# A decode step's last weight load cut into lines, and x added earlier on TensorE

## The chip, the cores and the metric

The kernel runs on one core of one Trainium2 chip, as one program. The metric is the device time of one execution in microseconds (us); the time of a kernel is the median of several executions. A separate, profiled execution gives the trace: which instruction ran when on which engine, when transfers were issued and when they landed, and the clock that TensorE was granted. TensorE does the matmuls, VectorE, ScalarE and GpSimd the elementwise work, and SyncE issues the transfers. Sixteen DMA engines carry them; a transfer is cut into packets, and each engine that takes part writes a closing packet of 4 bytes that counts up the transfer's semaphore.

## The reference

One decode step of two attention layers and two gated layers for a batch of 4 rows x of 512 numbers, all in bf16. Cut to what matters:

```python
def A(x, k_cache, v_cache, wq, wo):        # 32 query heads, 8 key heads, the last 2048 keys
    q = (x @ wq) split into heads
    p = softmax(q @ k.T * Dh ** -0.5)
    return (p @ v) joined @ wo

def B(x, w_gate, w_up, w_down):            # D = 512, F = 1792
    h = sigmoid(x @ w_gate) * (x @ w_up)
    return h @ w_down

x = x + A(layernorm(x)); x = x + B(layernorm(x))
x = x + A(layernorm(x)); x = x + B(layernorm(x))
```

Both rounds use the same caches and weights. The change lies in the last line's B: in the load of w_down, and in the place where x is added to h @ w_down.

## The kernel before, in words

The kernel writes down its work as a list of operations (`P.op`, line 52), each with its engine, an assumed duration, and the tiles that it reads and writes. `_schedule` (line 92) then gives each engine its order, by assumed times; in the second half of the program TensorE's operations keep the order in which they were written (`P.chain`, line 1622), and SyncE's transfers always do. `_assign_sync` (line 180) puts in the semaphore waits; the transfers go round 24 semaphores.

Nearly all transfers go from HBM into a large SBUF area, `arena`, cut into slots of 4 KB a partition. `load` and its kin append to a list of loads; `fill` issues from that list as soon as slots come free (`done`, line 469), and `need` (line 464) makes sure that a load has been issued before its user. The loads therefore run far ahead of the work, in one fixed order on one queue. The last ones are the gated layer's: two loads each of w_gate and w_up, and then w_down.

w_down has 1792 rows, laid out as 14 "lines" for each of 128 partitions (`wd_d`, line 319): partition p holds rows 14p to 14p + 13, and a block (a, b) of lines a to b - 1 is one transfer with one run of (b - a) KB for each partition. `bounds_of` (line 520) gives the blocks: in the last layer (0, 8), (8, 12) and (12, 14), in this order.

The last layer is `glu` with `last=True` (line 1445). Its steps, with their names:

- `glwg1_c` and `glwu1_c` (line 1484): for each quarter c of D, four matmuls of xn's 4 rows against 448 columns; quarters 0 and 1 come from the first load of the matrix, 2 and 3 from the second. The profile counts each of these pairs as 8 matmuls.
- gate and up are turned on VectorE (line 1496) and become hT, the transposed h (line 1518), by way of an exponential on ScalarE.
- `x_rows` (line 1457): GpSimd writes an identity into `prow` (line 1461), and four f32 matmuls (`xrow`, line 1468) write x's rows into the PSUM bank that will gather the result, with `start=True`. x is thus added by the accumulation.
- `kwI` (line 1522): two products of 448 columns into a bank that nobody reads. Such `keep_op`s (line 792) only keep TensorE busy.
- `gd1_a` (line 1533): for each line of a block four matmuls, one for each 128 columns, that add into that bank. Block (0, 8) has 32 of them, (8, 12) 16 and (12, 14) 8.
- four casts (line 1544), two on ScalarE and two on VectorE, and the transfer of the 4 result rows to HBM.

Of the kernel before, what the change touches and what calls it, by code (L numbers as in the profile page):

```python
# [254 lines left out]
class _SlotPool:  # L255
# [16 lines left out]
    bw_8k=421.0, bw_4k=409.0, bw_3k=405.0, bw_1k=347.0,  # L272
# [6 lines left out]
def build(nc, A_x, A_k, A_v, A_wq, A_wo, B_wg, B_wu, B_wd, out, cfg=None):  # L279
# [6 lines left out]
    NG = len(GROUPS)  # L286
# [38 lines left out]
    with es:  # L325
# [51 lines left out]
        def slot_ap(s):  # L377
            if s == SIDE:
                return side[:, 0:SLOT]
            return arena[:, s * SLOT:(s + 1) * SLOT]  # L380
# [7 lines left out]
        def tok(s):  # L388
            return [("slot", s), ("slot", s + 1)]
# [79 lines left out]
        def done(name):  # L469
            left[name] -= 1  # L470
            if left[name] == 0:
                s = where.pop(name)
                if name in on_free:
                    on_free[name](s)
                else:
                    pool.release(s)
                fill()
# [24 lines left out]
        def load(name, n_use, rate, part):  # L502
            left[name] = n_use

            def emit(s):
                src = part[1]
                dst = tile_ap(s)[:, 0:part[0]]
                if len(src.shape) == 3 and not part[2]:
                    dst = dst.rearrange("p (f n) -> p f n", f=src.shape[1])
                dma(str(name), dst, src, w=tok(s), rate=rate)  # L510
            loads.append((name, emit))
# [7 lines left out]

        def bounds_of(k):  # L520

            return [(0, 3), (3, 7), (7, 11), (11, NFC)] if k < NG else bounds[:-1] + [(bounds[-1][0], NFC - 2), (NFC - 2, NFC)]

        LAYERS = NG + 1

# [30 lines left out]
        def load_glu(k):  # L556
            for nm, src, two in (("wg", wg_d, wg_p), ("wu", wu_d, wu_p)):
                if k == 0:
                    for c in range(NC):
                        load_half((nm, c, k), src[:, c, :], "bw_3k", F,  # L560
                                  (((WR, 0), (Y, 0), (SP, 0), (Y, 1)), ((WQ, 0), (Z, 0), (WR, 0), (Y, 0)))[nm == "wu"][c])
                    continue
                for cc in range(NC // 2):
                    load((nm, cc, k), 2, "bw_8k", (2 * F, two[:, cc, :], False))
            for n, (a, b) in enumerate(bounds_of(k)):
                if k == 0:
                    load_half(("wd", a, k), wd_d[:, a:b, :].rearrange("p k n -> p (k n)"), "bw_4k", (b - a) * D,
                              ((SP, 0), (Y, 1), (WQ, 0), (Z, 0))[n])
                else:
                    load(("wd", a, k), 1, "bw_8k", ((b - a) * D, wd_d[:, a:b, :], False))  # L570


        STASH = SB + PBS
# [871 lines left out]
        def glu(k, b0, b1, add=None, last=False):  # L1445
# [11 lines left out]
            def x_rows():  # L1457
                xts = [("xT", b) for b in range(NB)]
                idf = prow[:, 256:512].bitcast(F32)
                P.op("gpsimd", "idf", 500.0,  # L1460
                     lambda g: g.affine_select(idf, one[:, 0:1].broadcast_to([128, 128]), [[1, 128]], ALU.is_equal, 0.0,
                                               base=0, channel_multiplier=-1),
                     r=[("one",)], w=[("prow",)])

                def e_x(pe):
                    last_ = None
                    for g in range(NC):
                        last_ = pe.matmul(ps[32 * g:32 * g + NB, PBS[0], 0:128], xT[:, g * NB:(g + 1) * NB], idf,
                                          start=True, stop=False, skip_group_check=True)
                    return last_  # L1470
                P.op("tensor", "xrow", 1200.0, e_x, r=xts + [("prow",)], w=[("orow",)], banks=(PBS[0],))
# [3 lines left out]
            for n, nm in enumerate(("wg", "wu")):  # L1475
                for c in range(NC):
                    name = (nm, c if k == 0 else c // 2, k)
                    s = need(name)

                    def e_g(pe, c=c, s=s, n=n):  # L1480
                        last = None
                        src = slot_ap(s) if k == 0 else tile_ap(s)[:, c % 2 * F:(c % 2 + 1) * F]
                        for g in range(4):
                            last = pe.matmul(ps[32 * g:32 * g + NB, gub[n], 0:NF], xn[:, c * NB:(c + 1) * NB],  # L1484
                                             src[:, g * NF:(g + 1) * NF], start=(c == 0), stop=(c == NC - 1),
                                             skip_group_check=True)
                        if k == 0 and c < NC - 1:
                            add_zeros(pe, 3 if c == 2 - 2 * n else 2, WB, NF)
                        return last
                    P.op("tensor", "gl%s%d_%d" % (nm, k, c), 4 * tm["pe_row"], e_g,  # L1490
                         r=(stok(s) if k == 0 else tok(s)) + [("xn",)], w=[("gu", n)], banks=(gub[n],))
                    done(name)
                if n == 0:
                    variance()
                P.op("vector", "gt%s%d" % (nm, k), c_dve(NF),
                     lambda v, n=n: v.transpose(ebuf[:, 0:NF],  # L1496
                                                ps[:, gub[n], 0:NF].rearrange("p (x k) -> p k x", k=NFC)),
                     r=[("gu", n)], w=[("e", 0), ("e", 1)], banks=(gub[n],))

                if n == 0:  # L1500
                    P.op("vector", "gs%d" % k, c_dve(NH),
                         lambda v: v.tensor_tensor(egv, tv, lnr[:, 0:nb].unsqueeze(1).broadcast_to([128, NFC, nb]), ALU.mult),
                         r=[("e", 0), ("e", 1), ("lnr", 0)], w=[("eg",), ("op", 0), ("op", 1)])
                    P.op("scalar", "gex%d" % k, c_act(NH),
                         lambda a: a.activation(eg[:, 0:NH], eg[:, 0:NH], ACTF.Exp, scale=-1.0),
                         r=[("eg",)], w=[("eg",)])
                    P.op("vector", "ga%d" % k, c_dve(NH),
                         lambda v: v.scalar_tensor_tensor(egv, egv, 1.0, lnd[:, 0:nb].unsqueeze(1).broadcast_to([128, NFC, nb]),
                                                          ALU.add, ALU.mult),
                         r=[("eg",), ("lnd",)], w=[("eg",)])  # L1510
                    P.op("vector", "gr%d" % k, c_dve(NH) + 60.0,
                         lambda v: v.reciprocal(eg[:, 0:NH], eg[:, 0:NH]), r=[("eg",)], w=[("eg",)])
# [5 lines left out]
                 lambda v: v.tensor_tensor(hT[:, 0:NH].rearrange("p (k b) -> p k b", b=NB), tv, egv, ALU.mult),  # L1518
                 r=[("e", 0), ("e", 1), ("eg",), ("op", 0), ("op", 1)], w=[("hT",)] + hts)
            if last:  # L1520
                x_rows()
                keep_op("kwI", 2, SB[0], 0, 448)
                for (a, b) in bounds_of(k):
                    name = ("wd", a, k)
                    s = need(name)

                    def e_d(pe, a=a, b=b, s=s):
                        last_ = None
                        src = tile_ap(s)
                        for fc in range(a, b):  # L1530
                            for g in range(NC):
                                o = (fc - a) * D + g * 128
                                last_ = pe.matmul(ps[32 * g:32 * g + NB, PBS[0], 0:128], hT[:, fc * NB:(fc + 1) * NB],
                                                  src[:, o:o + 128], start=False, stop=(fc == NFC - 1),
                                                  skip_group_check=True)
                        return last_
                    P.op("tensor", "gd%d_%d" % (k, a), (b - a) * 200.0, e_d,
                         r=tok(s) + [("hT",)] + hts, w=[("orow",)], banks=(PBS[0],))
                    done(name)
                orow = ebuf[0:NB, 0:half].bitcast(BF16)  # L1540
                for g in range(NC):
                    eng, f = ("scalar", "copy") if g % 2 == 0 else ("vector", "tensor_copy")
                    P.op(eng, "oc%d" % g, c_dve(128),
                         lambda e, g=g, f=f: getattr(e, f)(orow[:, g * 128:(g + 1) * 128], ps[32 * g:32 * g + NB, PBS[0], 0:128]),
                         r=[("orow",)], w=[("oc", g)], banks=() if g else (PBS[0],))
                dma("out", out_d, orow, w=[("out_dram",)], r=[("oc", g) for g in range(NC)], rate="bw_1k", nbytes=NB * D * 2,
                    sem=("out",))
                return
# [148 lines left out]
```

## Time and profile before

| what | value |
|---|---|
| median of 3 runs | 176.15 us (176.08 to 176.18) |
| profiled execution, its own time | 176.3 us |
| its span, first to last instruction | 174.6 us |
| TensorE (PE) busy | 114.9 us, 66% |
| VectorE (DVE) busy | 105.9 us, 61% |
| ScalarE (ACT), GpSimd (POOL) busy | 34.0 us, 23.1 us |
| read from HBM | 69.37 MB, 397 GB/s over the span |
| SyncE's transfer queue (q1) | 12344 packets, 97.0% of the 16 engines' span |
| mean granted TensorE clock | 0.98 |

How to read it: the profile's page cuts the span into 40 slices of 4.4 us and prints for each the busy share in tenths; the DMA row is the mean share of the 16 DMA engines, so that 0.32 means that about five of them work. The chain that ended last is followed back from the last instruction: each piece was released by the one in front of it. In a timeline row stand start, duration, engine, line, operation, the tiles written and read, and, in brackets, how long the engine idled before and what ended that. A matmul's duration contains its way through the array, so that matmuls in a row overlap.

### The profile page before, as it was taken

Reading aid. Unit: us, or ns where it says so; the run is one execution under the profiler, and the core shown is the slowest. Engines: PE = TensorE matmul, PEld = TensorE weight load, DVE = VectorE, ACT = ScalarE, POOL = GpSimd, SP = SyncE. Lnnn points to the kernel's source line nnn. Section 1 sums busy time; section 2 is a strip of 40 time slices with the busy share of each in tenths; the row PEclk is TensorE's granted clock in tenths of the full one; section 3 lists DMA queues with packets and bytes.
Section 4 is the critical chain, followed back from the end, with each engine's and each line's share of the span. In section 5 each row is a group of like instructions: output and inputs, shape, how many; then the busy total and the mean of one; then the engine's idle time right before and its main releaser. Section 6 shows DMA issues by size and latency. Waiting matters only on the chain.

```text
span 174.6 us, 3997 instructions
## 1 busy us (share of the span) xinstructions
PE 114.9 (66%) x1686; PEld 58.6 (34%) x1698; DVE 105.9 (61%) x262; ACT 34.0 (19%) x89; POOL 23.1 (13%) x92
## 2 busy tenths in 40 slices
PE   0536237167557092569788788767958999879853
PEld 0203012013434051243467552243323434446311
DVE  6407997994866938469323732316598999751531
ACT  2002022312212103011021010102233545430101
POOL 6100010101100101001010000002011543442000
PEclk9999999999999999999999999999999999999975
DMA  5999999999999999999999999999999999999970
GB/s 189 420 428 430 422 420 420 408 423 420 420 419 409 424 420 420 420 412 421 420 408 425 412 395 407 407 409 405 407 413 417 422 417 420 417 424 420 415 319 26
DMA packets 12370, 69.64 MB, mean 399 GB/s; under 512 B 1336, under 2 KB 1472, under 8 KB 6336
## 3 DMA queue, kind: packets, MB, share of 16 engines
q1 hardware_dynamic: 12344, 69.38, 97.0%
q8 instruction: 13, 0.21, 0.5%
q14 instruction: 5, 0.04, 0.1%
q10 hardware_dynamic: 8, 0.00, 0.0%
HBM read 69.37 MB, written 0.00 MB: 397 GB/s over the span
## 4 chain that ended last, share of the span: by engine, by line
DMA 71%; PE 11%; DVE 7%; SPq 6%; issue 1%; ACT 1%; POOL 0%; DVEq 0%
DMA arena<-in_A_v_cache_dram 49%; DMA arena<-in_B_w_down_dram 15%; SPq L400 6%; DMA side<-in_A_wq_dram 4%; DMA arena<-in_B_w_up_dram 4%; PE ps L783 2%; PE ps L1088 2%; DVE arena L595 1%; PE ps L986 1%; PE ps L1091 1%; PE ps L1181 1%; DVE small L1001 1%; ACT side L1016 1%; PE ps L1289 1%; DVE arena L1191 1%
## 5 line engine op out<-in xcount | busy, mean ns | idle before, releaser
L956 DVE STREAM_TRANSPOSE arena<-arena 128x1024 f32<-128x1024 f32 x32 | 37.0, 1205 | 0.1
L986 PE MATMUL ps<-arena,side 128*32 128x512 bf16 x256 | 23.3, 494 | 0.3
L1001 DVE TENSOR_REDUCE small<-ps 128x1 f32<-128x512 f32 x16 | 10.9, 679 | 15.8 <-PE ps L986 15.8
L783 PE MATMUL ps<-perm 128*128 128x448 bf16 (+1 forms) x65 | 18.5, 397 | 1.0 <-DVE side L1496 0.8
L1016 ACT ACTIVATE side<-ps,small 128x512 bf16<-128x512 f32 x16 | 11.0, 687 | 35.7 <-PE ps L1115 18.5
L973 PE MATMUL ps<-small,perm 128*128 128x512 bf16 x16 | 7.7, 482 | 12.0 <-DVE arena L956 11.3
L1088 PE MATMUL ps<-side,arena 128*128 128x64 bf16 x320 | 11.3, 192 | 4.0 <-DMA arena<-in_A_v_cache_dram 4.0
L1091 PE MATMUL ps<-side,arena 128*128 128x8 bf16 x256 | 8.1, 168 | 8.8 <-DMA arena<-in_A_v_cache_dram 8.7
L949 ACT CAST side<-ps 128x256 bf16<-128x256 f32 x16 | 5.9, 371 | 33.6 <-PE ps L986 26.6
L1088 PEld LDWEIGHTS ps<-side,arena 128*128 128x128 bf16 x320 | 10.2, 97 | 6.3 <-DMA arena<-in_A_v_cache_dram 6.3
L1031 ACT CAST side<-ps 128x512 bf16<-128x512 f32 x16 | 9.4, 587 | 12.6 <-PE ps L1289 2.9
L1045 POOL CAST small<-small 128x1 bf16<-128x1 f32 x9 | 1.7, 188 | 76.0 <-ACT side L1016 76.0
L1091 PEld LDWEIGHTS ps<-side,arena 128*128 128x128 bf16 x256 | 7.4, 104 | 11.6 <-DMA arena<-in_A_v_cache_dram 9.0
L986 PEld LDWEIGHTS ps<-arena,side 128*32 128x32 bf16 x256 | 6.3, 108 | 11.7 <-issue 8.7
L897 PE MATMUL ps<-arena,xn 128*4 128x512 bf16 x60 | 6.5, 498 | 4.2 <-DMA arena<-in_A_wq_dram 4.2
L1105 DVE TENSOR_TENSOR onb<-ps,rinv 128x16 bf16<-128x16 f32 x9 | 1.7, 185 | 11.4 <-PE ps L1088 10.8
L944 PE MATMUL ps<-side,eyew 32*128 32x64 bf16 x64 | 5.4, 212 | 4.3 <-ACT side L949 2.4
L1036 DVE STREAM_TRANSPOSE side<-side 128x256 f32<-128x256 f32 x16 | 6.9, 433 | 2.0 <-ACT side L1031 1.8
L1181 PE MATMUL ps<-arena,side 128*32 128x512 bf16 x112 | 7.3, 380 | 0.8 <-ACT side L1016 0.4
L783 PEld LDWEIGHTS ps<-perm 128*128 128x128 bf16 x65 | 5.9, 110 | 5.3 <-issue 2.9
L1496 DVE STREAM_TRANSPOSE side<-ps 128x448 f32<-128x448 f32 x4 | 2.6, 651 | 7.9 <-PE ps L1484 7.9
L1484 PE MATMUL ps<-arena,xn 128*4 128x448 bf16 x60 | 4.7, 360 | 3.1 <-DMA arena<-in_B_w_up_dram 2.7
(138 smaller groups left out, 151.1 us busy)
## 6 DMA issues: line engine op xcount, KB each, us to landing
arena<-in_A_v_cache_dram SPq DMA_DIRECT2D x26, 1024.0 KB, 16.6
arena<-in_A_k_cache_dram SPq DMA_DIRECT2D x16, 1024.0 KB, 24.9
arena<-in_A_wq_dram SPq DMA_DIRECT2D x4, 1024.0 KB, 7.8
arena<-in_A_wo_dram SPq DMA_DIRECT2D x3, 1024.0 KB, 26.6
arena<-in_A_v_cache_dram SPq DMA_DIRECT2D x5, 512.0 KB, 8.6
arena<-in_A_wq_dram SPq DMA_DIRECT2D x5, 512.0 KB, 6.7
arena<-in_B_w_up_dram SPq DMA_DIRECT2D x4, 448.0 KB, 6.1
arena<-in_B_w_gate_dram SPq DMA_DIRECT2D x2, 896.0 KB, 20.7
```

Source lines behind the costliest of these rows:

```text
L400: o = P.op("sync", name, 0.0, lambda e, dst=dst, src=src: e.dma_start(dst, src), r=r, w=w, dma_bytes=nbytes, dma_rate=tm[rate])
L783: last = pe.matmul(dst, weights, src, start=False, stop=False, skip_group_check=True)
L956: P.op("vector", "T%d_%d" % (h, t), c_dve(1024), lambda v, v32=v32: v.transpose(v32, v32), r=[("slot", 4 * h + t)], w=[("slot", 4 * h + t)])
L973: last = pe.matmul(ps[:, bank, :], perm[:, :], msk_m[:, :].unsqueeze(1).broadcast_to([128, 256, 2]), start=True, stop=False)
L986: last = pe.matmul(ps[32 * gi:32 * gi + 32, bank, :], qbd[:, q0:q0 + 32], kt[:, cp // 2, cp % 2, jh * NJ:(jh + 1) * NJ, :], start=False, s ...
L1001: lambda v: v.tensor_reduce(nmax[:, k2:k2 + 1], ps[:, bank, :], AXX, ALU.max),
L1016: lambda a: a.activation(prow[:, :].rearrange("p (m x t) -> p m x t", x=32, t=2), ps[:, bank, :].rearrange("p (m t x) -> p m x t", x=32, t ...
L1031: P.op("scalar", "pc" + tag, c_act(512), lambda a: a.copy(prow[:, :], ps[:, pb, :]), r=[("ppb", pb)], w=[("prow",)], banks=(pb,))
L1036: P.op("vector", "pt" + tag, c_dve(256), lambda v: v.transpose(et, prow[:, :].bitcast(F32)), r=[("prow",)], w=[("e", k2)])
L1088: last = pe.matmul(ps[:, ob, o:o + 64], v, ef[:, j % 2, at - at % 64:at - at % 64 + 64], start=(j == 0), stop=(j == 2 * NJ - 1), skip_grou ...
L1091: last = pe.matmul(ps[:, ob, bp * 8:bp * 8 + 8], v, ev[:, j % 2, j % 16 // 2, x0:x0 + 8], start=(j == 0), stop=(j == 2 * NJ - 1))
L1181: last = pe.matmul(ps[32 * g:32 * g + 32, ob, :], ew[:, g, mq, t], src.rearrange("p (m t d) -> p t m d", t=2, d=128)[:, t], start=(n == 0) ...
```

## The change

- The last layer's block (12, 14) becomes two blocks, (12, 13) and (13, 14), loaded in this order behind (8, 12).
- Block (13, 14) is loaded as two transfers: partitions 0 to 123 and partitions 124 to 127. The second has a token of its own, `wdb`, and takes over the first one's dependences, so that it waits for nothing else.
- TensorE works the blocks in the order (0, 8), (8, 12), (13, 14), (12, 13); the matmuls of line 13 wait for both of its parts.
- `x_rows` moves from behind hT to the place between the first and the second load of w_up, and four warm-keeping products (`kwJ`) go behind it.
- `kwI` has three products instead of two.

```diff
-            return [(0, 3), (3, 7), (7, 11), (11, NFC)] if k < NG else bounds[:-1] + [(bounds[-1][0], NFC - 2), (NFC - 2, NFC)]
+            return [(0, 3), (3, 7), (7, 11), (11, NFC)] if k < NG else bounds[:-1] + [(bounds[-1][0], NFC - 2), (NFC - 2, NFC - 1), (NFC - 1, NFC)]
...
+                elif b < NFC:
+                    load(("wd", a, k), 1, "bw_8k", ((b - a) * D, wd_d[:, a:b, :], False))
                 else:
-                    load(("wd", a, k), 1, "bw_8k", ((b - a) * D, wd_d[:, a:b, :], False))
+                    left["wd", a, k] = 1
+
+                    def emit(s):
+                        first = dma("wd%da" % a, slot_ap(s)[0:124, 0:D], wd_d[0:124, a, :], w=tok(s), rate="bw_1k")
+                        rest_ = dma("wd%db" % a, slot_ap(s)[124:128, 0:D], wd_d[124:128, a, :], w=[("wdb",)], rate="bw_1k")
+                        rest_.deps.update(first.deps)
+                    loads.append((("wd", a, k), emit))
...
                     done(name)
+                    if last and n and c == 1:
+                        x_rows()
+                        keep_op("kwJ", 4, SB[0], 0, 448)
...
             if last:
-                x_rows()
-                keep_op("kwI", 2, SB[0], 0, 448)
-                for (a, b) in bounds_of(k):
+                keep_op("kwI", 3, SB[0], 0, 448)
+                for (a, b) in bounds_of(k)[:-2] + bounds_of(k)[:-3:-1]:
...
-                                                  src[:, o:o + 128], start=False, stop=(fc == NFC - 1),
+                                                  src[:, o:o + 128], start=False, stop=(fc == NFC - 2),
...
-                         r=tok(s) + [("hT",)] + hts, w=[("orow",)], banks=(PBS[0],))
+                         r=tok(s) + [("wdb",)][:b == NFC] + [("hT",)] + hts, w=[("orow",)], banks=(PBS[0],))
```

## The prediction

> **What bounds the kernel now.** I read the head of the page first, then the chain that ended last from 140 us on, then the stretches around the end with their DMA share, then the timeline of the last ten microseconds.
>
> The page says that transfers fill the span, and that the queue which fetches instructions runs beside the loads:
>
> ```profile
> DMA  5999999999999999999999999999999999999970
> ...
> q1 hardware_dynamic: 12344, 69.38, 97.0%
> q8 instruction: 13, 0.21, 0.5%
> ...
> q10 hardware_dynamic: 8, 0.00, 0.0%
> ```
>
> The chain from 140 us on hangs on the w_down loads and then on the last 24 matmuls of line 1533:
>
> ```profile
> 144.13 26.99 DMA arena<-in_B_w_down_dram
> 171.12 0.04 issue
> 171.16 0.60 PE ps L1533 x16
> 171.76 0.04 issue
> 171.80 0.41 PE ps L1533 x8
> 172.21 0.02 issue
> 172.23 0.28 DVE side L1544
> ```
>
> The stretches (after the times come PE, PEld, DVE, ACT and POOL busy, granted clock, DMA share, GB/s) show how the transfers run out:
>
> ```profile
> 164.33:167.74 3.41, 1.65 (x30) 0.65 (x26) 1.59 (x4) 0.72 (x4) 0.00 (x0) 1.00 1.02 419
> ...
> 166.00:167.60 1.60, 0.14 (x4) 0.10 (x8) 0.72 (x2) 0.14 (x1) 0.00 (x0) 1.00 1.02 413
> 167.60:168.80 1.20, 1.20 (x17) 0.38 (x10) 0.61 (x1) 0.00 (x0) 0.00 (x0) 0.56 0.84 329
> 168.80:169.60 0.80, 0.64 (x2) 0.00 (x0) 0.26 (x2) 0.00 (x0) 0.00 (x0) 0.50 0.54 218
> 169.60:171.20 1.60, 1.06 (x36) 0.78 (x40) 0.00 (x0) 0.00 (x0) 0.00 (x0) 0.50 0.32 125
> ```
>
> From 169.6 to 171.2 the share is 0.32: about 5 of the 16 DMA engines still work while 11 are done. The trace records every completion. The 16 of load (8, 12) come at 167.98, 167.99, 168.11, 168.15, 168.44, 168.70, 169.22, 169.49, 169.51, 169.56, 169.71 and, for the late five, 170.93 to 171.12. Those of load (12, 14) end at 170.34 for eleven and 171.55 to 171.75 for the same five. The five are late because each carried two of the 13 instruction packets (16 KB, 1.02 to 1.11 us each, which move an engine's completions by about 1.5 us). So the last load is waited for on five engines, and the other eleven have 1.2 to 3.1 us to spare.
>
> The granted clock fell to half at 167.74, after a TensorE gap:
>
> ```profile
> 165.27 0.55 PE L1484 MATMUL ps<-arena,xn 128*4 128x448 bf16 x8
> ...
> 167.46 0.69 PE L1484 MATMUL ps<-arena,xn 128*4 128x448 bf16 x8 [1.64 <-DMA arena<-in_B_w_up_dram]
> ...
> 167.92 0.65 PE L1468 MATMUL ps<-side,xT 128*4 128x128 f32 x8
> ...
> 168.51 0.93 PE L783 MATMUL ps<-perm 128*128 128x448 bf16 x2
> ...
> 171.16 1.02 PE L1533 MATMUL ps<-arena,rinv 128*4 128x128 bf16 x24 [0.21 <-DMA arena<-in_B_w_down_dram]
> ...
> 172.91 0.34 SPq L400 DMA_DIRECT2D out_dram<-side  x1
> ```
>
> **The change, part by part.** The profiled execution took 176.3 us (span 174.6 and 1.7 around it); the three runs shown have a median of 176.15. I work in the span and take the saving off the median.
>
> *x and the warm-keeping matmuls.* The eight x passes took 0.65 us at half clock; four products of 448 columns took 0.93 us at full clock (the group at 152.93). Together at most 1.58 us; the gap from 165.82 to 167.46 holds 1.64. Should they run over by a tenth, the last up matmuls, the transpose (0.65) and hT (0.22) move by that tenth: hT stood ready at 169.10 and TensorE waited for load (0, 8) until 169.92, so 0.8 us of cover hides it. Taking x off its old place and making kwI three (at half clock 0.93 for two, so about 1.3) ends TensorE's work near 169.45, before 169.92. Cost zero, gain zero on the path; the identity that x needs was written by GpSimd at 155.97. What can come of it is the clock. The 3.41 us up to the fall had TensorE busy for 1.65; all such stretches before, back to 82.4 us, had 2.18 or more and kept full clock. With about 1.2 us more in it, this stretch has some 2.8, so the fall should not come at 167.74. But the next stretch, at full clock, has up matmuls 0.5, kwI 0.7 and the first w_down matmuls 0.6 and waits otherwise, again some 1.8 of 3.4: a fall before the last matmuls is as likely as not.
>
> In the Trainium skill, "TensorE: Matmul & The Clock Gate", section "What's actually happening", the gate watches a free-running window of 3413 ns. By it the fall lies elsewhere in each execution; the 3.41 us above agree, and the sum below holds for either clock.
>
> *The last load in parts.* A load of 128 lines gives each engine an equal share: the last one 8 packets of 2 KB, 80 ns from start to start. Line 12 alone is 8 packets of 1 KB; packets of 1 KB are seen only in the load of x, where the closing packet starts 40 ns after the data packet did. So the five late engines end 8 x 0.040 = 0.32 us earlier: 171.12 + 0.63 (now) becomes 171.12 + 0.32 = 171.44, if nothing of line 13 falls to them.
>
> How many engines take the 124 lines, no row of this trace shows. x's four lines made 8 packets on q10 (the row above), four of data and four closing ones: four engines, one line each. Bounds: spread over all 16, the late five carry 8 more packets (171.44 + 0.33 = 171.77, nothing gained); on four engines, each carries 31, 1.24 us. I take four, nearest to x's row.
>
> Which four decides. The first weight load starts on eight engines at 1.81 to 1.90 us, right behind x's packets, and on eight others at 2.60 or later. Of the first eight, four finish their first packet in 0.36 to 0.80 us and four in 1.11 to 1.23. I take the quick four to be those that had just carried x: two of them begin 11 ns after two of x's four closing packets end. Followed load by load through the completions, they stand at 168.44, 169.22, 169.49 and 169.71 at load (8, 12), none among the late five. The slowest then ends line 12 at 170.04, its 31 packets at 171.29, and its one packet of the 4-line part at 171.34: hidden behind 171.44, by only 0.1 us. Two further issues on SyncE (0.33 each) lie far ahead: its last load issue ended at 152.14, and only the output is queued behind them.
>
> The Trainium skill, "DMA: Bandwidth & Descriptors", section "Why a DMA increments its semaphore by 16 and not by 1", gives the largest divisor up to 16, on the lowest-numbered engines: four for 124 lines and the same four for 4. By its rule the sum is the one taken here; by an even spread it would be 176.2.
>
> *The end on TensorE.* The 16 matmuls of (8, 12) still start at 171.16. Behind them stand four of line 13 (they wait for both parts), then four of line 12. At half clock the rows give rounds of four at 107 ns and 0.31 for the last (8 took 0.41, 16 took 0.60, 32 took 1.02): six rounds make 5 x 0.107 + 0.31 = 0.85, ending at 172.01 instead of 172.21. At full clock a pair of weight load and matmul starts every 25 ns (16 in 0.55 at 157.20) and the last takes about 0.22: 23 x 0.025 + 0.22 = 0.80, ending at 171.96. So 0.20 to 0.25 us of the 0.31 that the loads give; the rest is lost because TensorE is now behind. The lower end is a gain of 0; the upper is 0.45, should the last matmuls start at 14 ns (the eight at the end of before) and wait for 171.49 alone. Casts, output and its landing follow unchanged.
>
> Sum: x and kwI 0; issues 0; loads -0.31; TensorE's backlog +0.08: -0.23. **176.15 - 0.23 = 175.92 us.**
>
> **The rivals.**
>
> *Both ends freed.* TensorE keeps full clock and its pairs go closer than 25 ns, so that the loads alone end it: 171.49 + 0.27 instead of 172.21, about 175.7. For it: the filled gap. Against it: the row of 25 ns, and the thin stretch from 168.7 on.
>
> *The split does nothing.* 124 lines go over all engines, or line 13's four engines end just after the late five and TensorE, which asks for line 13 first, holds line 12 behind it: 176.1 to 176.25. For it: my margin of 0.1 us, and TensorE's order. Against it: x's eight packets.
>
> *Slower: one of the four is a late one.* My identification rests on first-packet times and on following engines through crossings. If one of the late five carries line 13, its parts land at 171.12 + 0.32 + 1.25 + 0.06 = 172.75, the eight matmuls end at 172.79 + 0.41 = 173.20 instead of 172.21, and the time is 177.15. It begins to cost when one of the four completes load (8, 12) after 169.81, and costs over 0.2% from 170.48 on. A transfer on fewer engines does the same: on two, 62 packets take 2.5 us from 169.8 and end near 172.3, giving 176.6. For it: 31 packets on one engine are 1.24 us where eight took 0.64, five of sixteen engines are late, and no record here names an engine. Against it: the two starts right behind x's closing packets.
>
> **How the numbers follow.** The forecast has 0.50 (own range 175.78 to 176.1), both ends freed 0.15, nothing done 0.11, slower 0.24. 0.2% is 0.35 us, about what a measurement of this kernel can tell from no change. Faster than 175.80: 0.15 and 0.07 of the forecast's. Within: 0.43 and 0.11. Slower than 176.50: 0.24. The first three cases hold 0.76, so the range must reach into the slow case: 175.6 to 177.2.
>
> **What would show it.** Right: the late five completions of line 12 near 171.45, both parts of line 13 complete before that, on engines that were not late; in the stretch from 169.6 to 171.2 a DMA share of 0.4 to 0.55 rather than 0.32; x's matmuls at 165.9 and full clock past 167.74; the last matmul's end near 171.95. Wrong: a part of line 13 landing after 171.6 with TensorE's four matmuls waiting for it; sixteen completions spread for the 124 lines; or last matmuls that start with the landing at 171.49 and gain more than 0.35 us.

## The result, and the profile after

The changed kernel takes 176.55 us (median of 22 runs, 176.32 to 176.82), the kernel before, run beside it, 176.25 us (22 runs, 176.08 to 176.43). The ratio is 1.0016, with a 95% interval of 1.001 to 1.0023: slower by 0.30 us, where 0.23 us faster had been forecast. The time lies in the forecast's range of 175.6 to 177.2, but it moved the other way.

The profiled execution took 176.82 us (span 175.1, mean granted clock 0.986; before 176.3, 174.6 and 0.98). Its page, the rows of the clock, of the DMA share and of the queues:

```profile
PEclk9999999999999999999999999999999999999995
DMA  4999999999999999999999999999999999999970
...
q1 hardware_dynamic: 12480, 69.38, 96.6%
q8 instruction: 13, 0.21, 0.5%
```

The packet count says how many closing packets line 13 has. Block (12, 14) was 128 packets and 16 closing ones, 144. Line 12 alone is again 144. Line 13 is 128 packets of data and one closing packet for each engine of each part: with four engines for each part 4 + 4, so 136 more than before. 12344 + 136 = 12480, the number in the q1 row; the 124 lines spread over all sixteen would have made 12492. That the eight closing packets are four and four, the completions further down show.

The chain of the changed kernel that ended last, its end:

```profile
152.23 1.14 SPq L400
153.38 0.05 issue
153.42 18.75 DMA arena<-in_B_w_down_dram
172.17 0.14 issue
172.31 0.41 PE ps L1543 x8
172.74 0.28 DVE side L1554
173.02 0.33 DVEq L1666
```

It no longer runs through load (8, 12) and 16 matmuls: it hangs on one w_down transfer that lands at 172.17, and only eight matmuls follow. They start at 172.31, where the last eight of before started at 171.80; everything behind them is as long as it was. So the half microsecond between the two profiled executions lies in what lands last.

The stretches (after the times: PE, PEld, DVE, ACT and POOL busy, granted clock, DMA share, GB/s):

```profile
164.33:167.74 3.41, 2.77 (x46) 1.10 (x34) 1.58 (x4) 0.72 (x4) 0.00 (x0) 1.00 1.01 415
...
167.60:168.80 1.20, 1.16 (x11) 0.24 (x11) 0.65 (x1) 0.00 (x0) 0.00 (x0) 1.00 0.87 331
168.80:169.60 0.80, 0.00 (x0) 0.00 (x0) 0.22 (x1) 0.00 (x0) 0.00 (x0) 1.00 0.68 227
169.60:171.20 1.60, 1.02 (x32) 0.73 (x32) 0.00 (x0) 0.00 (x0) 0.00 (x0) 0.64 0.37 135
171.20:171.60 0.40, 0.06 (x5) 0.06 (x8) 0.00 (x0) 0.00 (x0) 0.00 (x0) 0.50 0.06 21
```

The clock is full to 168.80 and beyond, where it was 0.56 in the third of these stretches before. The DMA share is higher where three of line 13's engines work (0.68 against 0.54), and then hardly more than before: 0.37 against 0.32 from 169.60 on. From 171.20 to 171.60 it is 0.06: one engine of sixteen.

The timeline of the last ten microseconds:

```profile
165.72 0.39 PE L1476 MATMUL ps<-side,xT 128*4 128x128 f32 x8
...
166.04 0.93 PE L791 MATMUL ps<-perm 128*128 128x448 bf16 x4
...
167.53 0.55 PE L1492 MATMUL ps<-arena,xn 128*4 128x448 bf16 x8 [0.56 <-DMA arena<-in_B_w_up_dram]
...
168.02 0.74 PE L791 MATMUL ps<-perm 128*128 128x448 bf16 x3
...
170.17 1.02 PE L1543 MATMUL ps<-arena,rinv 128*4 128x128 bf16 x32 [1.41 <-DMA arena<-in_B_w_down_dram]
...
171.54 0.60 PE L1543 MATMUL ps<-arena,rinv 128*4 128x128 bf16 x16 [0.35 <-DMA arena<-in_B_w_down_dram]
...
172.31 0.38 PE L1543 MATMUL ps<-arena,rinv 128*4 128x128 bf16 x8 [0.17 <-DMA arena<-in_B_w_down_dram]
...
173.42 0.27 SPq L400 DMA_DIRECT2D out_dram<-side  x1
```

x's matmuls and the four products fill the gap in front of the last up piece, as the forecast had it. At the end TensorE is not behind: after the 16 matmuls of (8, 12) it waits again, and then works line 13 and line 12 together.

The completions, one for each engine that takes part, in order of time (us, from the trace); the bar stands in front of the late engines, of which one falls behind only between the first two rows:

```
load (0, 8)     166.85 166.86 166.99 167.05 167.34 167.35 167.38 168.01 168.19 168.24 168.32 168.90 | 169.84 169.87 170.11 170.12
load (8, 12)    168.14 168.15 168.27 168.34 168.62 168.63 168.67 169.29 169.54 169.60 170.43 | 171.00 171.05 171.22 171.32 171.49
line 12         168.49 168.50 168.59 168.66 168.99 169.04 169.09 169.71 169.94 170.00 170.73 | 171.29 171.51 171.52 171.76 171.77
line 13, 0-123  169.95 170.44 170.60 171.99
line 13, 124-   170.13 170.61 170.78 172.17
```

Four completions for each part. Three of the four engines are done long before the late five. The fourth is the eleventh in the row of load (8, 12), at 170.43 and not among the late five: its 31 packets start 42.5 ns apart, and 31 of these (1.32 us) before its completion at 171.99 lies 170.67, near the eleventh of line 12 at 170.73 and far from the tenth and the twelfth. Its one packet of the small part is counted at 172.17, 0.40 us behind the last of line 12.

### The profile page after: what moved, and what is told of

Same layout as the page of the kernel before. It is cut to its first block, busy times and chain, and to the rows that moved or that the text cites. A ratio compares the mean times of both kernels' runs of the same rounds, so it can differ in the third digit from the quotient of the medians.

```text
span 175.1 us, 4010 instructions
## 1 busy us (share of the span) xinstructions
PE 115.0 (66%) x1691; PEld 58.9 (34%) x1703; DVE 105.9 (60%) x262; ACT 33.9 (19%) x89; POOL 22.9 (13%) x92
## 3 DMA queue, kind: packets, MB, share of 16 engines
q1 hardware_dynamic: 12480, 69.38, 96.6%
## 4 chain that ended last, share of the span: by engine, by line
DMA 43%; DVE 31%; PE 20%; issue 2%; SPq 1%; ACT 1%; DVEq 0%
DMA arena<-in_A_v_cache_dram 19%; DVE arena L964 12%; DMA arena<-in_B_w_down_dram 11%; PE ps L994 7%; DMA arena<-in_A_wq_dram 6%; DVE small L1009 4%; DMA arena<-in_B_w_up_dram 4%; DMA side<-in_A_wq_dram 4%; PE ps L981 2%; DVE small L1013 2%; PE ps L791 2%; PE ps L1096 2%; DVE arena L1199 2%; DVE side L1044 2%; DVE side L1017 2%
## 5 line engine op out<-in xcount | busy, mean ns | idle before, releaser
L981 PEld LDWEIGHTS ps<-small,perm 128*128 128x128 bf16 x16 | 1.6, 100 | 13.9 <-DVE arena L964 12.6
```

The source lines that it names most:

```text
L981: last = pe.matmul(ps[:, bank, :], perm[:, :], msk_m[:, :].unsqueeze(1).broadcast_to([128, 256, 2]), start=True, stop=False)
```

## The experiments

The theory is that the loss is this fourth engine. Its rivals: the moved x and the extra products cost something; one more transfer with its wait costs by itself; the order on TensorE, line 13 ahead of line 12, holds finished work back. The later kernels vary how many engines share line 13. The table has the median, that of the kernel before measured beside it, the ratio with its interval, and from the profiled execution the last landings (us) of load (8, 12), of line 12 and of line 13.

| kernel | us | before | ratio (95%) | (8, 12) | line 12 | line 13 |
|---|---|---|---|---|---|---|
| changed kernel | 176.55 | 176.25 | 1.0016 (1.001 to 1.0023) | 171.49 | 171.77 | 172.17 |
| x_only | 176.33 | 176.29 | 1.0001 (0.9992 to 1.001) | 170.92 | 171.55, one block | 171.55, one block |
| split_only | 176.64 | 176.29 | 1.0018 (1.001 to 1.0027) | 171.30 | 171.70 | 172.05 |
| whole_lines | 176.24 | 176.29 | 0.9999 (0.999 to 1.0008) | 171.15 | 171.52 | 171.81 |
| line12_first | 176.46 | 176.29 | 1.0012 (1.0003 to 1.002) | 171.44 | 171.80 | 171.90 |
| four_early | 176.38 | 176.33 | 1.0004 (0.9994 to 1.0013) | 171.53 | 171.81 | 171.80 |
| cut_123 | 176.30 | 176.33 | 0.9999 (0.999 to 1.0008) | 171.40 | 171.68 | 171.41 |
| cut_123_12_first | 176.38 | 176.33 | 1.0003 (0.9993 to 1.0012) | 171.40 | 171.70 | 171.41 |
| cut_121 | 176.68 | 176.33 | 1.0022 (1.0013 to 1.0031) | 171.41 | 171.71 | 172.11 |
| cut_119 | 177.05 | 176.31 | 1.0035 (1.0023 to 1.0048) | 171.46 | 171.76 | 172.49 |

### x moved, w_down as before (x_only)

Against the kernel before, only the second half of the diff is kept:

```diff
+                    if last and n and c == 1:
+                        x_rows()
+                        keep_op("kwJ", 4, SB[0], 0, 448)
...
-                x_rows()
-                keep_op("kwI", 2, SB[0], 0, 448)
+                keep_op("kwI", 3, SB[0], 0, 448)
```

> Only x and the warm-keeping products are moved; w_down comes in its old three blocks. Theory L (the end is set by the slowest of the four engines that carry line 13): nothing is left of the loss, 176.2 to 176.3 beside a before of 176.25. Theory X (the earlier x passes and the seven products get in the way of the up matmuls): the loss of 0.3 us stays, 176.5 to 176.6.

176.33 against 176.29, neither a loss nor a gain that can be measured: the moved x is not the cause. The clock stayed full until 172.51 in the profiled execution, and the last eight matmuls start 0.05 behind the landing at 171.55, as before. The timeline of x_only:

```profile
167.75 0.74 PE L783 MATMUL ps<-perm 128*128 128x448 bf16 x3
...
169.80 0.62 PE L1535 MATMUL ps<-arena,rinv 128*4 128x128 bf16 x32 [1.31 <-DMA arena<-in_B_w_down_dram]
...
170.96 0.40 PE L1535 MATMUL ps<-arena,rinv 128*4 128x128 bf16 x16 [0.55 <-DMA arena<-in_B_w_down_dram]
...
171.60 0.28 PE L1535 MATMUL ps<-arena,rinv 128*4 128x128 bf16 x8 [0.24 <-DMA arena<-in_B_w_down_dram]
```

At full clock the matmuls are shorter (0.62 for 32 instead of 1.02), and then TensorE waits longer: the loads set this end.

### Only the cut of line 13 (split_only)

The first half of the diff alone; x and `kwI` stay as before:

```diff
+                        first = dma("wd%da" % a, slot_ap(s)[0:124, 0:D], wd_d[0:124, a, :], w=tok(s), rate="bw_1k")
+                        rest_ = dma("wd%db" % a, slot_ap(s)[124:128, 0:D], wd_d[124:128, a, :], w=[("wdb",)], rate="bw_1k")
...
                 x_rows()
                 keep_op("kwI", 2, SB[0], 0, 448)
+                for (a, b) in bounds_of(k)[:-2] + bounds_of(k)[:-3:-1]:
```

> Only w_down is cut into lines 12 and 13 (124 and 4 partitions), with TensorE's order of the change; x and kwI are where they were before. Theory L: the loss is here, 176.5 to 176.6, and the profile has one of line 13's four completions 0.2 to 0.6 us behind the last of line 12. Theory X: 176.2 to 176.3.

176.64 against 176.29, a ratio of 1.0018: the whole loss of the change. The parts of line 13 complete on four engines at 169.90, 170.58, 170.61, 171.87 and at 170.08, 170.75, 170.79, 172.05. The chain of split_only ends as that of the changed kernel does:

```profile
153.23 18.82 DMA arena<-in_B_w_down_dram
172.05 0.14 issue
172.18 0.41 PE ps L1541 x8
```

### Both lines whole (whole_lines)

As the changed kernel, with one more load and wait than before, but line 13 is one load of 128 partitions, and TensorE takes the blocks in the order of the loads:

```diff
-                        first = dma("wd%da" % a, slot_ap(s)[0:124, 0:D], wd_d[0:124, a, :], w=tok(s), rate="bw_1k")
-                        rest_ = dma("wd%db" % a, slot_ap(s)[124:128, 0:D], wd_d[124:128, a, :], w=[("wdb",)], rate="bw_1k")
...
-                for (a, b) in bounds_of(k)[:-2] + bounds_of(k)[:-3:-1]:
+                for (a, b) in bounds_of(k):
```

> As the change, but line 13 is one load of 128 partitions, so that every engine has 8 of its 1 KB packets, and TensorE takes line 12 first. Theory L: no engine carries more than another; the last landing comes 0 to 0.1 us behind that of before (16 packets of 1 KB, 42 ns each, in place of 8 of 2 KB, 80 ns each) and four matmuls are left behind it instead of eight (0.31 against 0.41 us): 176.15 to 176.3. A theory W, by which one more load and one more wait at the end cost by themselves, expects 176.4 or more.

176.24 against 176.29: one more load and wait cost nothing that can be measured. Line 12 lands at 171.52 and line 13 at 171.81, and two lines as two loads take as long as one block. The changed kernel has a further transfer, the small part; cut_123 below has it too, and no loss.

### Line 12 ahead of line 13 (line12_first)

```diff
-                for (a, b) in bounds_of(k)[:-2] + bounds_of(k)[:-3:-1]:
+                for (a, b) in bounds_of(k):
```

> As the change, but TensorE takes line 12 before line 13. Theory L: line 13 lands last (172.17 against 171.77 in the profile of the change), so four of the eight matmuls no longer wait for it: 0.1 us less than the change, 176.4 to 176.5. If line 12 were the late one, no gain or a loss of 0.1.

The ratio is 1.0012 where the change had 1.0016; the intervals overlap, so that the 0.1 us expected from the order is in keeping with the runs and not shown by them. By its interval, at least 0.0003 of loss stays with the order turned, so the order is no more than a part of the loss. In the profile both parts are in at 171.90, 0.10 behind line 12.

### A cut at 123 (cut_123, cut_123_12_first) and at 121 (cut_121)

The only edit in cut_123, and in cut_121 with 121 in its place; cut_123_12_first has the order of line12_first besides:

```diff
-                        first = dma("wd%da" % a, slot_ap(s)[0:124, 0:D], wd_d[0:124, a, :], w=tok(s), rate="bw_1k")
-                        rest_ = dma("wd%db" % a, slot_ap(s)[124:128, 0:D], wd_d[124:128, a, :], w=[("wdb",)], rate="bw_1k")
+                        first = dma("wd%da" % a, slot_ap(s)[0:123, 0:D], wd_d[0:123, a, :], w=tok(s), rate="bw_1k")
+                        rest_ = dma("wd%db" % a, slot_ap(s)[123:128, 0:D], wd_d[123:128, a, :], w=[("wdb",)], rate="bw_1k")
```

> As the change, but line 13 is cut into 123 and 5 partitions. By the rule that the change's four completions bear out (a load goes to as many engines as the largest divisor up to 16), 123 lines go to three engines, 41 packets of 42 ns each (1.74 us), and 5 lines to five. Theory L has two cases. If the late one of the change's four engines is the fourth, the three others end before the last of line 12 (169.95, 170.44 and 170.60 in the change, 0.43 later here), and the end falls back to line 12's own: 176.0 to 176.2 against 176.25 of before. If the late one is among the first three, line 13 lands 0.4 us later than in the change: 176.9 to 177.1.

The 123 lines have three completions (170.25, 171.01, 171.23) and the 5 lines five (168.93, 170.43, 170.65, 171.18, 171.41). Three of the five stand 0.17 to 0.18 behind the three. Of the other two, 170.65 stands 0.18 behind the eleventh completion of line 12 (170.47): the slow engine now has one packet of line 13 instead of 32. Each of the three now carries 41 packets instead of 31, and still all are done by 171.41, 0.27 ahead of line 12. So the late one of the four was the fourth, and without its share the loss is gone: 0.9999 against 1.0016, intervals apart. That shows the cause of the loss. Against the expectation of 176.0 to 176.2, nothing is gained over the kernel before. The timeline of cut_123, whose profiled execution (176.05 us) was its fastest:

```profile
171.44 0.51 PE L1543 MATMUL ps<-arena,rinv 128*4 128x128 bf16 x24 [0.88 <-DMA arena<-in_B_w_down_dram]
172.01 0.54 ACT L1554 CAST side<-ps 4x128 bf16<-4x128 f32 x2 [5.88 <-PE ps L1543]
```

TensorE's last 24 matmuls start at 171.44, when load (8, 12) is there; before it was 171.16. What the split gave to line 12 was taken from load (8, 12). The fast execution is no gain of the split: x_only, also at full clock to the last matmul and with the block of two lines whole, had its last matmuls done at 171.91 (0.31 from 171.60), cut_123 at 171.98 (0.54 from 171.44).

> Parts of 123 and 5 partitions, and TensorE takes line 12 first. If the three engines are free (theory L, late engine the fourth), line 13 is there before line 12 and the order costs nothing or up to 0.05 us against 123 with line 13 first: 176.0 to 176.2. If line 13 is late, four matmuls less wait behind it: 0.1 us under the run with 123 and line 13 first.

176.38 against 176.30, measured together, and both intervals contain 1: once the fourth engine is out, the order is worth nothing that can be measured. The 176.0 to 176.2 that was expected is missed here too.

> As the change, but line 13 is cut into 121 and 7 partitions: by the same rule eleven engines with 11 packets (0.47 us) and seven with one. It shows which of the sixteen completions of line 12 are those of the first eleven and of the first seven engines. Theory L: some of the five engines that fetch instructions are among the eleven (eight engines take turns at the fetches, and the engines that are free of them are eight), so that the last landing comes 0.5 us behind line 12's and the time is 176.5 to 176.8; if none of them is, 176.0 to 176.1.

The 121 lines have eleven completions, ten by 170.73 and one at 172.11; the 7 lines have seven, all by 170.84. So one of the first eleven engines is one of the late five, and 11 packets behind its share of line 12 it ends the kernel: 1.0022.

### The small part ahead (four_early)

The 4 lines are loaded in front of line 12, the 124 lines behind it, and TensorE takes line 12 first:

```diff
+                        rest_ = dma("wd%db" % a, slot_ap(s)[124:128, 0:D], wd_d[124:128, a, :], w=tok(s), rate="bw_1k")
...
+                        dma("wd%d" % (a - 1), tile_ap(s)[:, 0:D], wd_d[:, a - 1, :], w=tok(s), rate="bw_1k")
...
+                        first = dma("wd%da" % a, slot_ap(t)[0:124, 0:D], wd_d[0:124, a, :], w=[("wdb",)], rate="bw_1k")
```

> As the change with line 12 first on TensorE, but the load of 4 partitions of line 13 is issued ahead of line 12 instead of behind the 124. Theory L: the slowest engine has the same 41 packets in all, so only the last closing step goes: in the change the 4-partition part lands 0.18 us behind the 124 on every one of the four engines. 0.1 to 0.2 us less than with line 12 first and the old order of parts (176.46): 176.25 to 176.4. If the closing steps cost nothing, 176.45.

176.38, a ratio of 1.0004. The 124 lines end at 171.80, together with line 12; the 0.18 us between the two parts is off the end. The loss can no longer be told from none, but the interval overlaps that of line12_first (1.0012), so that a gain from the order of the parts is not shown.

### A cut at 119 (cut_119)

As cut_123, with 119 and 9 partitions.

> As the changed kernel, but line 13 comes as parts of 119 and 9 partitions. The 11, 7, 3, 5 and 4 completions seen so far let me expect 7 completions for the 119-part (17 packets each instead of 31) and 9 for the 9-part. Theory (the length of the fourth engine's share set the loss): the fourth engine's part lands 14 packets x 42 ns = 0.6 us earlier than the 171.9 of the split kernels, near 171.3, so ahead of line 12's last landing at 171.5 to 171.7, and the loss of 0.3 us is gone; the time is between the kernel before and 0.2 us below it, because line 12 on the late five engines and TensorE's backlog then set the end as with 123 and 5 partitions. Theory (any uneven last load stretches the other engines' packets): load (8, 12) and line 12 land as late as in the changed kernel, line 12 past 171.7, and nothing is gained. A result within 0.1 us of the kernel before fits both; the landings tell them apart. Rival (two transfers of small parts cost by themselves): 0.2 us or more above the kernel before.

A miss: 177.05 against 176.31. There are seven completions for the 119 lines and nine for the 9, as expected, and six of the seven are done by 171.07, the fourth engine's part among them (its line 12 was at 170.38, so it had 17 packets and 0.69 us). The seventh comes at 172.29 and its packet of the small part at 172.49. It stands on one of the late five, whose line 12 ended between 171.25 and 171.76: 17 packets of 42.5 ns are 0.72 us behind that. The timeline of cut_119:

```profile
171.50 0.60 PE L1543 MATMUL ps<-arena,rinv 128*4 128x128 bf16 x16 [0.22 <-DMA arena<-in_B_w_down_dram]
...
172.62 0.38 PE L1543 MATMUL ps<-arena,rinv 128*4 128x128 bf16 x8 [0.52 <-DMA arena<-in_B_w_down_dram]
```

In cut_121 none of the seven engines of the small part was late. If the 119 lines went to the same seven, one of these was late in this execution. One of the six executions of cut_119 took 176.47 and the others 176.97 to 177.24. Whether the late five are different engines from one execution to the next was not tried; under that condition the two traces show that they were not the same ones.

No version beat the kernel before.

## Why the prediction was wrong, point by point

**x and the warm-keeping matmuls: right.** Forecast zero; x_only measured a ratio of 1.0001. The fall of the clock at 167.74 stayed away, and the clock fell at 170.04 instead, before the last matmuls. Two stretches of the changed kernel (columns as above) up to that fall:

```profile
163.22:166.63 3.41, 3.09 (x47) 1.52 (x47) 1.74 (x8) 0.72 (x4) 0.00 (x0) 1.00 1.01 420
166.63:170.04 3.41, 1.57 (x13) 0.31 (x11) 1.27 (x3) 0.00 (x0) 0.00 (x0) 1.00 0.80 305
```

TensorE was busy for 1.57 of the 3.41 us before the fall, near the 1.65 that preceded it in the kernel before and near the 1.8 that the forecast gave for this stretch. In all eleven profiles the full clock, up to its last fall, lasted a whole number of such stretches, 25, 26 or 27 of 3413 ns; the last of them had TensorE busy for 1.13 to 1.67 us, and all the others for 1.95 or more. The window of 3413 ns in the Trainium skill ("TensorE: Matmul & The Clock Gate", section "What's actually happening") agrees with this. The clock is no part of the difference between the two profiled executions: the last eight matmuls ran at half clock in both, for 0.41 us, where x_only has 0.31 at full clock.

**The two more issues on SyncE: free, as forecast.** They were not 0.33 us each: the chain above has 1.14 us for the 124 lines, and the issue of the 4 lines took 7.68 us, to 161.10. The output alone is queued behind them, twelve microseconds later, so the size did not matter.

**Four engines: right.** Four completions for each part. The Trainium skill's rule of the largest divisor ("DMA: Bandwidth & Descriptors", section "Why a DMA increments its semaphore by 16 and not by 1") held for every cut: 124 and 4 lines had 4 and 4 completions, 123 and 5 had 3 and 5, 121 and 7 had 11 and 7, 119 and 9 had 7 and 9.

**"None among the late five": right for the four.** Three of them ended at 169.95, 170.44 and 170.60, where the forecast's way gives 170.02, 170.80 and 171.07. They were up to 0.47 earlier, so that the forecast's identification of these three engines is not borne out one by one.

**"The slowest then ends line 12 at 170.04, its 31 packets at 171.29, and its one packet of the 4-line part at 171.34: hidden behind 171.44, by only 0.1 us": this is the step that failed.** The mechanism, 31 packets behind the fourth engine's share of line 12, was the right one; the term was mis-sized, above all the time at which that engine has done load (8, 12). Measured were 170.73, 171.99 and 172.17, 0.83 us later than forecast:

- Load (8, 12) on that engine came at 170.43 instead of 169.71, +0.72. Of this, 0.16 is the whole execution (its first completion is at 168.14, before at 167.98).
- The engine's lag behind the first one was already 2.05 at load (0, 8), where the eleventh of before had 1.76: +0.29. This lag belongs to the execution: it was 2.03 to 2.06 at every load of the changed kernel from 145 us on and 1.72 to 1.78 in the kernel before from 133 us on, and over the eleven profiles it was 1.76 to 2.28 at load (0, 8).
- Between the two loads the lag grew by 0.24, where it had shrunk by 0.03: +0.27. This part comes with the uneven load. From load (0, 8) to load (8, 12) the slowest engine ahead of the late ones took 1.23 to 1.25 us in the three kernels whose last loads are even, with the same share for every engine (before, x_only, whole_lines), and 1.47 to 1.62 in the eight with an uneven last one. The forecast took the time from the kernel before and put what line 13 does to the packets in front of it at nothing, without a reason.
- Line 12 took 0.30 instead of 0.33, the 31 packets 1.26 instead of 1.25: right, -0.02 together.
- The 4-line part was counted 0.18 behind the other one, not 0.05: +0.13. Its closing packet itself starts 0.05 behind that of the other part (171.52 and 171.57 in the trace); the two are counted 0.47 and 0.60 later.

One profile gave me a completion time for an engine, and I used it to the hundredth against a margin of 0.1. In the other kernels with even loads the same lag at load (8, 12) is 1.85 (x_only) and 1.84 (whole_lines), already enough to use up the margin. The lag differs between executions by more than the margin; the forecast had that as a rival's condition, not as the spread of its own term. The line that it was to hide behind, line 12 on the late five, came 0.33 later as well (171.77 instead of 171.44). With this and the margin of 0.1 taken off, 0.40 us of the 0.83 stood out.

**Loads -0.31: not there.** Line 12 alone is as quick as forecast: its last completion comes 0.28 us after the last of load (8, 12) (forecast 0.32, before 0.63 for the block of two lines). But load (8, 12) itself ends at 171.49, not 171.12, so that line 12 ends at 171.77, where the block of before ended at 171.75. It is no accident of one execution: on the late five, load (8, 12) ended at 170.92 to 171.15 in the three kernels whose loads are even and at 171.30 to 171.53 in the eight with an uneven last one. (A part of that stands already at load (0, 8), with 169.75 to 169.93 against 169.90 to 170.25.) cut_123 shows what this leaves of the forecast without the fourth engine: a ratio of 0.9999, where 0.9987 had been forecast for the change (175.92 / 176.15).

**The end on TensorE, +0.08: did not come about in the changed kernel,** because the last transfer is later than the backlog. In cut_123 24 matmuls run from the landing of (8, 12) on, but its last four start at 171.73 only, 0.05 behind the landing of line 12, so that backlog and load end together there. The forecast's price at full clock was too high: it took 25 ns for a matmul from a row with weights of 128 columns, 0.80 us for the 24, and here 24 took 0.51, four of them every 55 ns.

**The rivals.** The slower one names the mechanism that decided, on another engine. Its condition "begins to cost when one of the four completes load (8, 12) after 169.81" was met, at 170.43, by an engine that is not one of the late five; by its own terms that gives a landing at 170.43 + 0.33 + 1.25 + 0.06 = 172.07, where 172.17 was measured. Its price of 177.15 is for 31 packets behind a late engine, and no run has that. cut_119 comes nearest, with 17: by the same terms its last part would land near 172.2 and the time be about 176.6, but 172.49 and 177.05 were measured, so that the likeness of 177.05 and 177.15 is chance. "Both ends freed" had its condition on TensorE met at full clock (14 ns for a matmul instead of 25), but not the one on the loads: line 12 landed at 171.68 at the earliest where line 13 was uneven, not at 171.44, and no kernel came near 175.7; the five executions of cut_123 with the fullest clock took 176.05 to 176.19. The prediction's own sign of failure, "a part of line 13 landing after 171.6 with TensorE's four matmuls waiting for it", is what the chain shows.

From the landings to the time: the last transfer at 172.17 instead of 171.75 is +0.42, the wait for it ended 0.14 instead of 0.05 behind it, +0.09, and the eight matmuls, casts and output are unchanged. That is +0.51, against +0.52 between the two profiled executions. The medians are only 0.30 apart: this execution was the slowest of its 22, and its loads stood 0.13 to 0.16 later from 160 us on. The profiled execution of split_only lies nearer its median (176.67 and 176.64); there the last transfer is 0.30 later than before and the wait again 0.09 longer, +0.39, against +0.37 between the executions.

## What to carry to other kernels

Work moved from all DMA engines to a few is as late as the slowest of these few at that moment, so take its finishing time as a range over several executions, and ask for a margin of the size of that range. Several loads of one profile do not give it: there the lag of the fourth engine hardly moved (1.72 to 1.78 us in the kernel before), and between the eleven profiles it was 1.76 to 2.28. A part whose number of lines has few divisors concentrates: look up how many engines share it by its closing packets, and price a late one among them. And allow for what the uneven load does to the load in front of it: on the fourth engine that load took 1.5 us instead of 1.24, and on the late five it lost what line 12 had gained.

## What the runs showed of the hardware

**An uneven load makes the packets beside it longer.** From 168.75 to 170.5 us, packets of 4 KB (load (8, 12)) lasted 159 ns in the median in the kernels with even loads, and over 165 ns were 0 of 46 (before), 2 of 44 (x_only) and 3 of 49 (whole_lines). With line 13 cut unevenly they were 26 of 43 (changed kernel), 29 of 41 (split_only), 18 of 37, 25 of 39, 16 of 41, 32 of 41, 9 of 37 and 26 of 44 in the order of the table. Packets of 1 KB in that time were 46 ns each in whole_lines, up to 84 in the changed kernel and up to 102 in others. The bytes are the same; what slows them was not found, and no run here was made for it.

**Two parts on the same engines are counted 0.17 to 0.20 us apart,** although the second has one packet for each engine. This is read by pairing the completions of the two parts, and holds in every cut where the small part was issued behind the large one.

**The clock may decide where TensorE has the last word.** Of cut_123's ten executions, the five with a mean granted clock of 0.993 or more took 176.05 to 176.19 us, the five with 0.991 or less 176.40 to 176.62. With cut_123_12_first no such order is seen, and so it stays a hint: 24 matmuls took 0.51 us at full clock in cut_123 and 0.77 in the profiled execution of the other, from the same 171.44.
